# Sparse attention and two dense layers on one core: shifting every SBUF tile to a multiple of 128 bytes

## The chip, the cores and the metric

The kernel runs on one core of one Trainium2 chip. The metric is device time in microseconds (us) of one execution, the median of several runs. TensorE multiplies, VectorE, ScalarE and GpSimd do elementwise work, and SyncE issues almost all transfers. A profile names them PE, DVE, ACT, POOL and SP; PEld is TensorE loading the stationary operand of the next matmul.

## The reference

Attention over 4 batches of 8 heads (576 rows of 64), in which only scores within tau of the row's largest take part, is followed by two dense blocks on the 2304 rows of 512.

```python
scores = scale * np.matmul(q, k.transpose(0, 1, 3, 2))
thresh = np.max(scores, axis=-1, keepdims=True) - tau
scores = np.where(scores >= thresh, scores, -1000000000.0)
attn = softmax(scores)                    # exp, sum + 1e-9, divide
x = np.matmul(attn, v)                    # to rows of 512
h = x @ w_in                              # 512 -> 2048
g = np.maximum(h, 0.0) + alpha * np.minimum(h, 0.0)
x = g @ w_out                             # 2048 -> 512
h = ((x @ w1) * (x @ w2)) @ w3            # 512 -> 1024, 1024 -> 1024
out = h @ w_out2                          # 1024 -> 512
```

The weights arrive as 64-bit floats, and the kernel converts them to 32-bit ones on the chip.

## The kernel before

**Stages.** The attention goes over 16 pairs of heads. For a pair, q and k are loaded (L229, L233), split into a high and a low part (L140, L144, L147, tiles `qs` and `ks`), transposed (L258, L264) into `qT` and `kT`, and `qT` is copied with its halves swapped into `qU` by a transfer (L298). Nine groups of 128 rows follow: four matmuls of 288 columns each (L321), row maximum (L336), exponential (L345), mask (L357), scaling (L380), transposes (L403), and the product with v (L428). Meanwhile 14 of the 16 slices of `w_in` are converted.

The dense part works on five tiles of rows of `x`: four of 512 columns and one of 256, the order being tile 0, the tile of 256, tiles 1 to 3. Every product is made of three matmuls (high by high, high by low, low by high), all by `mm_group` (L819), in a type of 4 bytes that passes through TensorE once. `h<-x,wa` in a profile means that the moving operand is `x` and the stationary one is `wa`; so also `acc<-gs,wu` (second product of the first block), `h<-wu,x` (the product of w3 and w_out2, made once), and `acc<-wp,gs` (the last product). While the first three tiles run, DVE, ACT and POOL convert the other weights (L155 to L177) and put 40 slices of them to DRAM and back.

**Order.** The order of all instructions is made ahead of time by a planner, `list_order`, from estimated costs, and it is fixed in the program: each engine takes its instructions in that order and waits by semaphores. The change leaves the planner and its costs alone.

**Where the tiles lie.** A pool takes a stretch of SBUF from the left or from the right end of what is free, and each tile in it is rounded up to 32 bytes of a partition. Every large tile is a multiple of 128 bytes long, so what stands ahead of the first one sets the remainder of all on that side. On the left the small tiles of `const` (`ident` to `kscale`, L125 to L132) take 1312 bytes from 16512 on, so `xT0` starts at 17824 = 139 x 128 + 32 and the 16 `wa` tiles at 54688 = 427 x 128 + 32, and so on. On the right the free part ends at 229344 = 1791 x 128 + 96, so all tiles of the pools `att`, `dn` and `wu` (`qT`, `kT`, `qU`, `pt`, `x`, `gs`, `wu`, `wp`) start 96 bytes past a multiple of 128. Two operands are at a multiple of 128 already: `ident` (16512) and `ident_r` (17024), the moving operands of the transposes. Between the two sides 576 bytes are free in the dense part, and more than that in the attention.

Of the kernel before, what the change touches and what calls it, by code (L numbers as in the profile page):

```python
# [9 lines left out]
F32 = mybir.dt.float32  # L10
# [73 lines left out]
def kernel(  # L84
# [25 lines left out]
    nc = tc.nc  # L110
# [13 lines left out]
    const = ctx.enter_context(tc.tile_pool(name="const", bufs=1))  # L124
# [7 lines left out]
    kscale = const.tile([128, 1], F32, name="kscale")  # L132

    tiles = [SM] * B + [B * ST]
    xT = [const.tile([128, KD, n], F32, name=f"xT{t}") for t, n in enumerate(tiles)]
    w_a = ctx.enter_context(tc.tile_pool(name="w_a", bufs=16, reuse_waits="tile"))

# [41 lines left out]

    with tc.manual_schedule():  # L180
        make_identity(nc, ident)
        nc.scalar.dma_start(out=tau_sb, in_=tau.partition_broadcast(128))
        nc.scalar.dma_start(out=alpha_sb, in_=alpha.rearrange("(c p) -> p c", p=128))
        nc.vector.tensor_copy(ident_r, ident)
# [905 lines left out]
```

## Time and profile before

| | us |
|---|---|
| median of 3 runs | 1103.19 (1102.81 to 1104.49) |
| the profiled execution, its own time | 1106.0 |
| its span, first to last instruction | 1104.2 |
| PE busy | 1064.2 (96%) |
| DVE busy | 713.5 (65%) |

The span is what the profile's rows add up to; 1.8 us of the profiled execution's time lie around it. The end of a matmul is modelled in the profile, and matmuls overlap, so the distance from the start of one run of matmuls to the start of the next, divided by their number, tells what one costs.

### The profile page before, as it was taken

The page shows a single profiled execution, that of the slowest core. Times are in us where ns is not written, and L with a number is a line of the kernel's source. Part 1 is how long each engine was busy: PE and PEld are TensorE (multiplying, and loading weights), DVE is VectorE, ACT ScalarE, POOL GpSimd, SP SyncE. Part 2 cuts the span into 40 slices and gives each one's busy share as a digit, 9 for nine tenths or more (in the row PEclk, how much of TensorE's full clock was granted, in tenths as well). Part 3 has the DMA queues.
Part 4 walks back from the last instruction along what each step waited for, and adds up shares of the span by engine and source line. Part 5 has one row for each costly group of instructions (what it writes and reads, how often), then busy time and mean ns, then how long its engine had stood idle before and what let it go on. Part 6 is the DMA issues. An engine that isn't in the chain of part 4 may idle for free.

```text
span 1104.2 us, 17783 instructions
## 1 busy us (share of the span) xinstructions
PE 1064.2 (96%) x6464; PEld 891.1 (81%) x6464; DVE 713.5 (65%) x1425; ACT 438.7 (40%) x875; POOL 439.4 (40%) x679
## 2 busy tenths in 40 slices
PE   5999999999999998999989999999999999999997
PEld 5888888888878778978867788888888888888886
DVE  4999999999979999888666635654322312323122
ACT  4888888888874433332333212211110101111020
POOL 5888888888843444454343102301200101000000
PEclk9999999999999998999989999999999999999999
DMA  6443343343213335555434301323100100001010
GB/s 157 123 118 101 102 123 100 107 107 79 60 40 115 108 102 160 175 165 170 124 124 138 101 1 38 97 76 96 48 1 1 39 1 10 29 1 39 1 39 20
DMA packets 62392, 89.25 MB, mean 81 GB/s; under 512 B 13920, under 2 KB 42592, under 8 KB 62304
## 3 DMA queue, kind: packets, MB, share of 16 engines
q1 hardware_dynamic: 60096, 88.10, 27.0%
q8 instruction: 51, 0.84, 0.3%
q10 hardware_dynamic: 2208, 0.01, 0.1%
q14 instruction: 37, 0.30, 0.1%
HBM read 62.40 MB, written 15.20 MB: 70 GB/s over the span
## 4 chain that ended last, share of the span: by engine, by line
PE 65%; DVE 16%; POOL 8%; issue 5%; DMA 3%; ACT 2%; SPq 0%; POOLq 0%; DVEq 0%; ACTq 0%
PE h L819 33%; PE acc L819 21%; POOL p L380 4%; PE s_ps L321 3%; PE pt_ps L403 3%; PE pv_ps L428 3%; DVE p L357 2%; DVE m L172 2%; DVE sm L336 2%; DVE m L168 2%; DMA raw<-in_moe_w_dram 2%; DVE m L166 1%; POOL m L177 1%; DVE g L891 1%; DVE m L163 1%
## 5 line engine op out<-in xcount | busy, mean ns | idle before, releaser
L819 PE MATMUL h<-x,wa 128*128 128x512 f32 (+1 forms) x1920 | 419.7, 371 | 2.7 <-DVE x L147 1.3
L819 PEld LDWEIGHTS h<-x,wa 128*128 128x128 f32 x1920 | 336.0, 189 | 67.9 <-POOL x L147 2.4
L819 PE MATMUL acc<-gs,wu 128*128 128x512 f32 (+1 forms) x960 | 216.8, 374 | 10.7 <-POOL gs L147 5.2
L819 PEld LDWEIGHTS acc<-gs,wu 128*128 128x128 f32 x960 | 169.1, 190 | 47.2 <-POOL gs L147 8.9
L1011 DVE TENSOR_TENSOR ab<-h,ab 128x512 f32<-128x512 f32 (+1 forms) x40 | 25.5, 638 | 207.6 <-PE h L819 201.0
L147 POOL TENSOR_TENSOR x<-xT,x 128x512 fp32r<-128x512 f32 (+1 forms) x18 | 21.6, 1208 | 296.8 <-ACT x L142 249.3
L177 POOL TENSOR_TENSOR m<-m,raw 128x512 int32<-128x512 int32 x58 | 79.4, 1369 | 121.2 <-DVE m L172 90.4
L345 ACT ACTIVATE e<-s_ps,sm 128x576 f32<-128x576 f32 x144 | 108.0, 750 | 37.3 <-DVE sm L336 35.3
L336 DVE TENSOR_REDUCE sm<-s_ps 128x1 f32<-128x576 f32 x144 | 106.0, 744 | 7.3 <-PE s_ps L321 6.9
L1008 ACT COPY ab<-h 128x512 f32<-128x512 f32 (+1 forms) x38 | 20.6, 542 | 223.0 <-PE h L819 220.5
L380 POOL TENSOR_SCALAR p<-p,sm 128x576 f32<-128x576 f32 x128 | 102.9, 808 | 14.4 <-DVE sm L373 10.9
L357 DVE SCALAR_TENSOR_TENSOR p<-s_ps,sm,e 128x576 f32<-128x576 f32 x128 | 103.2, 807 | 6.8 <-ACT e L345 5.1
L819 PE MATMUL acc<-wp,gs 128*128 128x512 f32 x432 | 104.6, 389 | 0.9 <-DVE gs L144 0.9
L886 ACT ACTIVATE g<-h,sign_sb 128x512 f32<-128x512 f32 (+1 forms) x80 | 51.3, 641 | 115.0 <-PE h L819 100.4
L403 PE MATMUL pt_ps<-ident,p 128*128 128x128 f32 x576 | 91.3, 281 | 3.9 <-issue 2.7
L819 PEld LDWEIGHTS acc<-wp,gs 128*128 128x128 f32 x432 | 80.3, 188 | 17.6 <-DVE gs L144 1.1
L428 PE MATMUL pv_ps<-pt,vraw 128*64 128x128 f32 (+1 forms) x1280 | 92.5, 291 | 0.1
L321 PE MATMUL s_ps<-kT,qT 128*128 128x288 f32 x320 | 83.4, 343 | 2.6 <-DVE p L357 1.7
L428 PEld LDWEIGHTS pv_ps<-pt,vraw 128*64 128x64 f32 x1280 | 73.0, 136 | 11.9 <-ACT e L345 4.7
L403 PEld LDWEIGHTS pt_ps<-ident,p 128*128 128x128 f32 x576 | 66.0, 141 | 19.1 <-POOL sm L339 9.2
L891 DVE SCALAR_TENSOR_TENSOR g<-h,salpha_sb,g 128x512 f32<-128x512 f32 (+1 forms) x80 | 55.4, 693 | 39.9 <-ACT g L886 39.7
L415 ACT COPY pt<-pt_ps 128x512 f32<-128x512 f32 x128 | 76.1, 595 | 12.7 <-PE pt_ps L403 10.7
(109 smaller groups left out, 1324.7 us busy)
## 6 DMA issues: line engine op xcount, KB each, us to landing
raw<-in_moe_w_dram SPq DMA_DIRECT2D x32, 512.0 KB, 3.9
raw<-in_moe_w_out_dram SPq DMA_DIRECT2D x24, 512.0 KB, 3.6
qU<-qT SPq DMA_DIRECT2D x32, 320.0 KB, 4.2
z<-w SPq DMA_DIRECT2D x40, 256.0 KB, 2.7
wraw<-in_moe_w_in_dram SPq DMA_DIRECT2D x14, 512.0 KB, 3.8
w<-m SPq DMA_DIRECT2D x24, 256.0 KB, 2.2
qraw<-in_q_dram SPq DMA_DIRECT2D x16, 256.0 KB, 3.2
kraw<-in_k_dram SPq DMA_DIRECT2D x16, 256.0 KB, 2.9
```

What stands on the lines that cost most here:

```text
L177: nc.gpsimd.tensor_tensor(out=mc[0], in0=mc[0], in1=mc[1], op=ALU.add)
L321: nc.tensor.matmul(out=sp[:, j, 0:HS], lhsT=d[t][:, hh, c * 128 : (c + 1) * 128], rhs=d["kT"][:, hh, k0 + j * HS : k0 + (j + 1) * HS], sta ...
L336: nc.vector.tensor_reduce(out=sm[u][:, 0:1], in_=st[u], axis=AX.XY, op=ALU.max, negate=True)
L345: nc.scalar.activation(out=es[u].rearrange("p (j s) -> p j s", j=2), in_=st[u], func=AF.Exp, bias=sm[u][:, 0:1])
L357: nc.vector.scalar_tensor_tensor(out=p.rearrange("p (j s) -> p j s", j=2), in0=st.pop(u), scalar=sm[u][:, 1:2], in1=es.pop(u).rearrange("p ...
L380: nc.gpsimd.tensor_scalar(out=out, in0=in_, scalar1=r, scalar2=1.0, op0=ALU.mult, op1=ALU.mult)
L403: nc.tensor.transpose(t[:, i, :], p[:, at + i * 128 : at + (i + 1) * 128], ident)
L415: nc.scalar.copy(out=pt[:, g, 0:4, 0:128], in_=ps)
L428: nc.tensor.matmul(out=o[64 * hh : 64 * hh + 64, 0:n], lhsT=vr[:, hh, i, :], rhs=pt[:, 0 if i == 4 and c < 3 else hh, i, 0:n], start=(i == 0),
L819: nc.tensor.matmul(out=out, lhsT=l, rhs=r, start=first and i == 0, stop=last and i == n - 1)
L886: nc.scalar.activation(out=gt()[:, 0:n], in_=ps()[:, 0:n], func=AF.Copy, scale=sign_sb[:, f : f + 1])
L891: nc.vector.scalar_tensor_tensor(out=gt()[:, 0:n], in0=ps()[:, 0:n], scalar=salpha_sb[:, f : f + 1], in1=gt()[:, 0:n], op0=ALU.mult, op1=A ...
```

## The change

A tile of 24 elements of 4 bytes, 96 bytes of a partition, that nothing uses is put behind the small tiles of `const`, and a second one, in a pool of its own, at the right end. So the left tiles start 96 bytes later and the right ones 96 bytes earlier: `xT0` at 17920 = 140 x 128, the `wa` tiles from 54784 = 428 x 128 on, and the right side ends at 229248 = 1791 x 128. The right gap is set to zero once, by a GpSimd instruction behind the making of `ident`.

```diff
     tiles = [SM] * B + [B * ST]
+    const.tile([128, 24], F32, name="gap")
+    edge = ctx.enter_context(tc.tile_pool(name="edge", bufs=1, side="right"))
+    gap = edge.tile([128, 24], F32, name="gap_r")
     xT = [const.tile([128, KD, n], F32, name=f"xT{t}") for t, n in enumerate(tiles)]
...
         make_identity(nc, ident)
+        nc.gpsimd.memset(gap, 0.0)
         nc.scalar.dma_start(out=tau_sb, in_=tau.partition_broadcast(128))
```

## Rows read from the trace of the kernel before

**Rows 1.** The page, busy us (share of the span) and instructions of TensorE.

```profile
PE   1064.2 (96%) x6464; PEld 891.1 (81%) x6464; DVE 713.5 (65%) x1425; ACT 438.7 (40%) x875; POOL 439.4 (40%) x679
```

**Rows 2.** Windows: busy us (x instructions) of each engine, granted clock, DMA.

```profile
30.00:327.00 297.00, 291.80 (x2793) 248.95 (x2791) 279.94 (x719) 248.56 (x551) 250.53 (x501) 1.00 0.36 96
327.00:472.00 145.00, 135.74 (x743) 115.38 (x742) 135.30 (x210) 60.36 (x107) 63.42 (x48) 0.98 0.42 131
472.00:630.00 158.00, 150.97 (x680) 121.74 (x681) 113.76 (x176) 49.32 (x81) 64.56 (x48) 0.98 0.44 139
630.00:1090.00 460.00, 460.00 (x2099) 382.25 (x2098) 165.41 (x273) 64.76 (x110) 42.52 (x30) 1.00 0.10 31
```

**Rows 3.** The chain that ended last, 30 to 327 us, by line.

```profile
by line: POOL p L380 14.9%; issue 13.3%; PE pv_ps L428 10.7%; PE s_ps L321 10.7%; PE pt_ps L403 10.4%; DVE p L357 7.8%; DVE sm L336 6.7%; DVE praw L357 3.2%; POOL sm L368 2.9%; POOL ks L140 2.8%; PE tr L264 2.6%; ACT e L345 2.4%; POOL qs L1
```

**Rows 4.** The chain, 327 to 472 us, by line.

```profile
by line: DMA raw<-in_moe_w_dram 13.1%; DVE m L172 12.9%; DVE m L168 9.6%; issue 9.4%; DVE m L166 9.3%; DVE wu L719 8.2%; DVE m L163 7.6%; DVE g L891 7.1%; POOL m L177 7.1%; DVE gs L147 4.6%; DVE gs L144 2.3%; DVE x L147 2.0%; DVE wa L144 1.
```

**Rows 5.** The chain, 472 to 630 us, by line.

```profile
by line: PE h L819 41.5%; PE acc L819 38.7%; PE h L748 4.5%; POOL m L177 2.7%; DVE g L891 1.9%; issue 1.6%; DVE m L166 1.4%; POOL gs L147 1.3%; DVE m L172 1.3%; DVE x L147 1.1%; ACT g L886 0.9%; DVE gs L144 0.9%; DVE m L168 0.8%; DVE m L163
```

**Rows 6.** The chain, 630 to 1090 us, by line.

```profile
by line: PE h L819 65.0%; PE acc L819 35.1%
```

**Rows 7.** Timeline of TensorE, 716 to 731 us: start, us, group.

```profile
722.15 2.88 PE L819 MATMUL acc<-gs,wu 128*128 128x512 f32 x12
724.87 2.91 PE L819 MATMUL h<-x,wa 128*128 128x512 f32 x12
727.62 2.88 PE L819 MATMUL acc<-gs,wu 128*128 128x512 f32 x12
```

**Rows 8.** Timeline of TensorE, 745 to 790 us.

```profile
754.93 5.60 PE L819 MATMUL h<-wu,x 128*128 128x512 f32 x24
760.37 2.88 PE L819 MATMUL acc<-gs,wu 128*128 128x512 f32 x12
```

**Rows 9.** Timeline of TensorE, 434.5 to 440 us, the tile of 256.

```profile
434.42 1.52 PE L819 MATMUL h<-x,wa 128*128 128x256 f32 x12
435.78 1.60 PE L819 MATMUL acc<-gs,wu 128*128 128x256 f32 x12
437.22 1.52 PE L819 MATMUL h<-x,wa 128*128 128x256 f32 x12
```

**Rows 10.** Timeline of TensorE, 140 to 160 us, the scores.

```profile
146.08 0.43 PE L321 MATMUL s_ps<-kT,qT 128*128 128x288 f32 x2
146.35 0.43 PE L321 MATMUL s_ps<-kT,qU 128*128 128x288 f32 x2
146.62 0.60 PE L403 MATMUL pt_ps<-ident,p 128*128 128x128 f32 x4
```

**Rows 11.** Groups by form, TensorE, 472 us to the end: count, busy us, mean ns.

```profile
L819 PE MATMUL h<-x,wa 128*128 128x512 f32 x1344 | 324.5, 395 | 1.7 <-DVE x L147 1.3 <-POOL x L147 0.3
L819 PE MATMUL acc<-gs,wu 128*128 128x512 f32 x576 | 139.1, 391 | 2.0 <-DVE gs L144 1.1 <-POOL gs L147 0.6 <-DVE gs L147 0.2
L819 PE MATMUL acc<-wp,gs 128*128 128x512 f32 x432 | 104.6, 389 | 0.9 <-DVE gs L144 0.9
L819 PE MATMUL h<-wu,x 128*128 128x512 f32 x192 | 43.8, 389 | 0.0
L819 PE MATMUL h<-x,wa 128*128 128x256 f32 x192 | 24.0, 279 | 0.0
```

**Rows 12.** Timeline of TensorE, 1064 to 1076 us, the last tile.

```profile
1066.87 5.81 PE L819 MATMUL h<-x,wa 128*128 128x256 f32 x48
1072.52 1.53 PE L819 MATMUL acc<-wp,gs 128*128 128x512 f32 x6
```

**Rows 13.** Instructions that write `gs` and `x`: ns min/median/max.

```profile
L144 DVE CAST gs<-g x59: 280/429/1541, 336.5 to 752.7; 128x512 fp32r<-128x512 f32 x51, 128x256 fp32r<-128x256 f32 x8
...
L144 DVE CAST x<-xT x19: 282/421/1267, 321.0 to 1059.5; 128x512 fp32r<-128x512 f32 x16, 128x256 fp32r<-128x256 f32 x3
```

**Rows 14.** Timeline of GpSimd, 0 to 22 us: start, us, group, idle before.

```profile
1.36 0.15 POOL L207 MEMSET qraw<- 64x64 f32 x1
...
6.48 0.46 POOL L140 TENSOR_SCALAR qs<-qraw 128x320 fp32r<-128x320 f32 x1 [2.19 <-DMA qraw<-in_q_dram]
```

## The prediction

> **What bounds the kernel.** The page first: TensorE is busy for 96% of the span [rows 1], so what a matmul costs matters, if it is TensorE that sets the end. That differs by stage, so I read windows next and the chain of waits for each. From 30 to 327 us (attention) DVE is nearly as full as PE, 280 us and 292 us of 297 [rows 2], and the chain goes through all engines: the PE lines named there (L428, L321, L403, L264) have 34.4% of it, the scores' matmuls (L321) 10.7% [rows 3]. From 327 to 472 us, in which the first tile and the tile of 256 run, no PE line stands in the part of the chain that is shown: it is the conversion of weights on DVE (135 of 145 us busy [rows 2]) and the loads of weights, 13.1% [rows 4]. From 472 to 630 us PE has 41.5 + 38.7 + 4.5 = 84.7% [rows 5], and from 630 to 1090 us everything [rows 6], at a granted clock of 1.00, the 2.4 GHz level [rows 2]. So a cheaper matmul counts in full over 460 us, mostly over 158 us, and hardly before.
>
> Then I read what one matmul costs, as starts of neighbouring runs. With 512 columns, `acc<-gs,wu` takes (724.87 - 722.15) / 12 = 226.7 ns, `h<-x,wa` 2.75 / 12 = 229.2 ns [rows 7], and `h<-wu,x` 5.44 / 24 = 226.7 ns [rows 8]. With 256 columns, `acc<-gs,wu` takes 1.44 / 12 = 120.0 ns, `h<-x,wa` 1.36 / 12 = 113.3 ns [rows 9] and, in the last tile, 5.65 / 48 = 117.7 ns [rows 12]. The scores' matmuls of 288 columns take 0.54 / 4 = 135 ns [rows 10]. At 2.4 GHz, 226.7 ns is 544 cycles, 120.0 ns is 288, and 135 ns is 324: 32, 32 and 36 more than there are columns.
>
> **Where those 32 cycles may come from.** Columns are 4 bytes wide. A moving operand of 512 columns that starts 96 bytes past a multiple of 128 touches 17 stretches of 128 bytes, where an aligned one would touch 16; 17 times 32 columns is 544. With 256 columns it touches 9 (288 cycles), with 288 columns 10 (320). If a matmul pays for whole stretches, all three sizes come out, and the change removes one stretch from each. But a fixed 32 cycles per matmul, say for handing over the stationary operand, fits the three sizes too. What tips me is a pair: `h<-x,wa` and `h<-wu,x` have the same three passes, the same length and the same kind of output bank, and differ in where the operands lie; in the second both start 96 past, in the first `wa` starts 32 past. Yet they differ, 229.2 against 226.7 ns [rows 7, 8], and with 256 columns `h<-x,wa` differs from `acc<-gs,wu` the other way, 113.3 against 120.0 ns [rows 9]. So time on TensorE does seem to depend on the place within 128 bytes, which the change alters for every operand of the dense products.
>
> The rows show 226.7 ns for 512 columns. The Trainium skill, TensorE: Matmul & The Clock Gate, in its section "Wait — 56ns, not 53.3ns?", gives 215.7 ns for back-to-back matmuls of 512 columns at full clock; this trace does not agree, it is 11.0 ns dearer. By that page the gain per matmul of 512 columns could be 11.0 ns, which changes the sum below by under 1 us.
>
> **The change, part by part.** Nothing in the order of instructions moves, and no wait or transfer is added or taken away.
>
> - The memset of the right gap: one more on GpSimd, behind `ident`. One of 64x64 takes 0.15 us [rows 14]. GpSimd idles 2.19 us before its first work on `qs` [rows 14], waiting for q to land, so I cost it at 0; without that cover it is 0.15 us.
> - Elementwise work: `gs<-g`, whose two tiles start equally far past, and `x<-xT`, whose tiles start 64 bytes apart, have medians of 429 and 421 ns [rows 13]. So I give DVE, ACT and POOL nothing. A gain on DVE would show most before 472 us; the 8 ns between the two medians, over the 929 DVE instructions of 30 to 472 us [rows 2], bound it at 7 us either way.
> - Transfers: the wait for weights is 13.1% of 145 us, 19 us [rows 4]. If shifted destinations made those transfers cheaper or dearer by a tenth, it is 2 us either way; I take 0.
> - Matmuls from 472 us to the end [rows 11]: 576 + 432 + 192 = 1200 at 226.7 ns, 1344 `h<-x,wa` at 229.2 ns, and 192 of 256 columns at 117.7 ns. Between nothing and the 13.3 ns of the 32 cycles I take 10.7 ns, leaving a fifth for a hand-over that no row shows apart. 1200 x 10.7 ns = 12.8 us. For `h<-x,wa` the 2.5 ns that it has beyond the others go too: 1344 x 13.2 ns = 17.7 us. The 256-column ones fall to 106.7 + 2.6 = 109.3 ns: 192 x 8.4 ns = 1.6 us. Together 32.1 us.
> - What of it is lost: a quarter of those 632 us is the stretch from 472 to 630, so 8.0 us of the gain. What is late next there are the conversions that PE already waits for, 15.3% of the chain [rows 5], and a faster PE comes to them sooner. I take off a quarter, 2.0 us; the bounds are 0 and 8.0 us.
> - Matmuls from 327 to 472 us: 743 of them [rows 2], at most 743 x 10.7 ns = 7.9 us. DVE and the loads set the end there [rows 4], so I take 0.
> - Scores: 40 matmuls in each of 16 pairs. Their 10.7% of 297 us on the chain is 32 us [rows 3]; 10.7 of 135 ns is 8%, so 2.5 us at most. I take 1.0 us, since another engine is close behind.
>
> Sum: 32.1 - 2.0 + 1.0 = 31.1 us. The profiled execution took 1106.0 us, so 1074.9 us; it is 2.8 us above the median of 1103.2, so I give 1072 us for the median.
>
> **Rivals.**
>
> - Half a stretch. The 113.3 ns of `h<-x,wa` are 272 cycles, 256 + 16 [rows 9], as if the unit were 64 bytes, and all operands now start 32 past a multiple of 64. Then one unit of 16 cycles, 6.7 ns, goes: 1200 x 6.7 + 1344 x 6.7 + 192 x 6.7 = 18.3 us, 1.2 us lost before 630 us, so 1086 us. Against it: no run of 512 columns in the rows stands at 528 cycles.
> - Only the step between the two operands matters. Then 32 cycles per matmul stay, and `h<-x,wa` comes down to the others, since afterwards all start at the same place: 1344 x 2.5 = 3.4 us less, and 192 x (120.0 - 117.7) = 0.4 us more, so 1100 us. For it speaks that three pairs of operands in step all show 226.7 ns [rows 7, 8].
> - The change does not do what it says, as to time. All tiles already start at multiples of 32 bytes, and if SBUF is read in pieces that divide 32, no piece is saved; the 32 cycles are then a hand-over, and the 2.5 ns of `h<-x,wa` have to do with which pool the operand is in. Then 1103 us. The Trainium skill, SBUF — State Buffer, under "Specifications (TRN2)", speaks for it: it gives cachelines of 16 bytes, at whose multiples all tiles stand before and after. The trace does not clearly agree: `wa`, 32 past, and `wu`, 96 past, are both on such lines, and differ by 2.5 ns.
> - Slower: moving and stationary operands that start at the same multiple of 128 get in each other's way. In step at 96 past they show 226.7 ns, so nothing yet speaks for it; the price is bounded by what being out of step costs now, 2.5 ns. On the 1200 matmuls that lack it, that is 3.0 us, so 1106 us; it decides from 1.8 ns on, 2.2 us. One more stretch for each would be 2736 x 13.3 ns = 36 us.
>
> **How the numbers follow.** About 0.2%, 2.2 us, is what can be told from no change. Full stretch 0.48, half a stretch 0.17, step alone 0.10, nothing 0.15, slower 0.10. The step alone lies at -3 us, so 0.06 of it counts as faster and 0.04 as same. Faster is 0.48 + 0.17 + 0.06 = 0.71, same 0.04 + 0.15 = 0.19, slower 0.10. The likeliest case by itself reaches from 1063 us (all 13.3 ns gone, 7.1 us more, and nothing lost before 630 us) to 1079 us (all 8.0 us lost and no gain at the scores). The range is 1063 to 1103.5 us: it holds nearly all of the first, the next two, and about half of no change, some 0.8.
>
> **What would show it right or wrong.** Right: runs of 512 columns at 214 to 217 ns in the timeline, equal for `h<-x,wa`, `h<-wu,x` and `acc`; 256 columns at 107 to 110 ns, 288 at 121 to 125 ns; the first 472 us nearly as long as before, with more idle PE from 327 to 472 us. A pitch of 220 ns says half a stretch, 226.7 everywhere says step alone. If pitches fall and the span does not, the bound has moved to the conversions, and PE's idle time before L819 grows by what was saved. The forecast fails most simply if 32 cycles stay.

## The result: 0.6% slower

The changed kernel takes 1110.78 us (median of 5 runs, 1110.36 to 1111.24) against 1104.49 us for the kernel before in the same series; the ratio is 1.0057, with a 95% interval of 1.0040 to 1.0074. The profiled execution took 1110.9 us, with a span of 1109.1 us, 4.9 us more than before. Each engine's instructions stand in the same order as before, with the one memset added.

The page of the changed kernel, TensorE's line, as [rows 1]:

```profile
PE   1071.5 (97%) x6464; PEld 892.5 (80%) x6464; DVE 714.0 (64%) x1425; ACT 439.3 (40%) x875; POOL 439.6 (40%) x680
```

PE has the same 6464 matmuls and is busy 7.3 us longer; DVE, ACT and POOL have changed by less than 1 us. Next the last two of the windows, as [rows 2]: us, busy us (x instructions) of PE, PEld, DVE, ACT and POOL, granted clock, DMA.

```profile
472.00:630.00 158.00, 152.23 (x681) 122.12 (x681) 114.21 (x174) 49.22 (x80) 63.24 (x47) 0.98 0.42 139
630.00:1090.00 460.00, 460.00 (x2057) 377.86 (x2057) 163.73 (x269) 63.90 (x108) 42.44 (x30) 1.00 0.10 31
```

The granted clock is that of before in all four windows of [rows 2]. In the three up to 630 us as many matmuls are done as before, to within 3 (2790, 746 and 681). In the 460 us in which nothing but PE stands on the chain, 2057 matmuls fit where 2099 did [rows 2], so on average one got dearer. Which ones did, the timeline of TensorE tells (start, us, group), as [rows 7, 8 and 12]:

```profile
622.32 5.82 PE L823 MATMUL h<-x,wa 128*128 128x512 f32 x24
...
719.53 2.96 PE L823 MATMUL h<-x,wa 128*128 128x512 f32 x12
722.33 2.92 PE L823 MATMUL acc<-gs,wu 128*128 128x512 f32 x12
725.08 2.96 PE L823 MATMUL h<-x,wa 128*128 128x512 f32 x12
...
750.09 5.63 PE L823 MATMUL acc<-gs,wu 128*128 128x512 f32 x24
755.56 5.60 PE L823 MATMUL h<-wu,x 128*128 128x512 f32 x24
761.00 2.88 PE L823 MATMUL acc<-gs,wu 128*128 128x512 f32 x12
...
921.27 2.90 PE L823 MATMUL acc<-wp,gs 128*128 128x512 f32 x12
924.01 5.75 PE L823 MATMUL h<-x,wa 128*128 128x512 f32 x24
...
1071.24 5.93 PE L823 MATMUL h<-x,wa 128*128 128x256 f32 x48
1077.01 1.56 PE L823 MATMUL acc<-wp,gs 128*128 128x512 f32 x6
...
1102.22 1.66 PE L823 MATMUL acc<-wp,gs 128*128 128x512 f32 x6 [0.91 <-DVE gs L147]
```

The same view of the kernel before, where [rows 7, 8 and 12] do not show it:

```profile
623.61 5.75 PE L819 MATMUL h<-x,wa 128*128 128x512 f32 x24
...
918.97 2.88 PE L819 MATMUL acc<-wp,gs 128*128 128x512 f32 x12
921.69 5.66 PE L819 MATMUL h<-x,wa 128*128 128x512 f32 x24
927.18 2.88 PE L819 MATMUL acc<-wp,gs 128*128 128x512 f32 x12
...
1097.29 1.66 PE L819 MATMUL acc<-wp,gs 128*128 128x512 f32 x6 [0.92 <-DVE gs L144]
```

Starts are printed to 0.01 us, so the pitch (the time from one matmul's start to the next) is known to 0.8 ns from a run of 12 and to 0.4 ns from one of 24; less than that is not read. From start to start, `h<-x,wa` went from 229.2 to (722.33 - 719.53) / 12 = 233.3 ns, and with 256 columns from 117.7 to 5.77 / 48 = 120.2 ns. `h<-wu,x`, whose operands now both start at a multiple of 128, is at 5.44 / 24 = 226.7 ns, where it was. `acc<-gs,wu` went from 226.7 to 2.75 / 12 = 229.2 ns, but in a run of 24 it is at 5.47 / 24 = 227.9 ns: some 30 ns per run, however long it is. It is paid where `acc` follows a run of `h<-x,wa`, and is not `acc`'s own: between two runs of `h<-wu,x`, from 761.00 to 763.72 us, `acc<-gs,wu` is at 226.7 ns.

This accounts for the time. From the start of a run of 24 `h<-x,wa` (623.61 us before, 622.32 us now; it stands on the chain in both) to that of TensorE's last run (1097.29 and 1102.22 us), called the *tail* below, it was 473.7 us and is 479.9 us: 6.2 us more, as the medians say (6.3 us). That the run starts 1.3 us earlier now says nothing of the change: in both_shift below, which has the pitches of before, it starts at 619.58 us, and in right_only at 624.30 us. In the tail of before are 1056 `h<-x,wa` of 512 columns (x 4.1 ns = 4.3 us), 300 `acc<-gs,wu` (x 2.5 = 0.8), 432 `acc<-wp,gs` (2.74 / 12 = 228.3 now, 226.7 before; x 1.6 = 0.7) and 192 `h<-x,wa` of 256 columns (x 2.5 = 0.5): 6.3 us together.

### The profile page after: what moved, and what is told of

Its sections match the earlier page's. It is cut to its first block, busy times and chain, and to the rows that moved or that the text cites. A ratio compares the mean times of both kernels' runs of the same rounds, so it can differ in the third digit from the quotient of the medians.

```text
span 1109.1 us, 17784 instructions
## 1 busy us (share of the span) xinstructions
PE 1071.5 (97%) x6464; PEld 892.5 (80%) x6464; DVE 714.0 (64%) x1425; ACT 439.3 (40%) x875; POOL 439.6 (40%) x680
## 4 chain that ended last, share of the span: by engine, by line
PE 61%; DVE 17%; POOL 9%; issue 6%; DMA 4%; ACT 3%; SPq 0%; POOLq 0%; DVEq 0%; ACTq 0%
PE h L823 33%; PE acc L823 20%; POOL p L384 4%; DMA raw<-in_moe_w_dram 3%; DVE p L361 3%; PE s_ps L325 2%; PE pv_ps L432 2%; DVE sm L340 2%; PE pt_ps L407 2%; DVE m L175 2%; DVE m L171 2%; POOL m L180 2%; DVE m L169 2%; DVE g L895 1%; DVE wu L723 1%
## 5 line engine op out<-in xcount | busy, mean ns | idle before, releaser
L823 PE MATMUL h<-x,wa 128*128 128x512 f32 (+1 forms) x1920 | 426.4, 375 | 2.6 <-DVE x L150 1.3
```

The source lines that it names most:

```text
L823: nc.tensor.matmul(out=out, lhsT=l, rhs=r, start=first and i == 0, stop=last and i == n - 1)
```

## The experiments

Two theories, and the names that the expectations use: D, the pitch of a matmul depends on the *distance* between the places of its moving and its stationary operand; P, it depends on the *place* of an operand within 128 bytes. In bytes, x - wa (for the `wa` tile at the lowest place) was 139840 = 546 x 256 + 64 before, and is 139648 = 545 x 256 + 128 after; gs - wu, wp - gs and wu - x are multiples of 256 in both.

**staircase.** Each `wa` tile is 32 bytes longer than it needs to be, so that the 16 tiles lie at 16 distances, 8 of them different modulo 256.

```diff
-            wa[f] = w_a.tile([128, 2, KD, 128], F32R, tag="wa", name="wa")
+            w = w_a.tile([128, 1032], F32R, tag="wa", name="wa")
+            wa[f] = w[:, 0:1024].rearrange("p (a k f) -> p a k f", a=2, k=KD)
...
-                box["w"] = pool.tile([128, 2, 512], F32R, tag=tag, name=tag, **kw)
+                if pool is w_a:
+                    w = pool.tile([128, 1032], F32R, tag=tag, name=tag, **kw)
+                    box["w"] = w[:, 0:1024].rearrange("p (a f) -> p a f", a=2)
+                else:
+                    box["w"] = pool.tile([128, 2, 512], F32R, tag=tag, name=tag, **kw)
```

> Each stationary tile of w_in lies 32 bytes further from the one ahead of it than before, so slice f starts 576 - 32f bytes below x (modulo 4096); x, gs, wu and wp stay where they were. Theory D (what counts is the distance between the moving and the stationary operand): the pitch of h<-x,wa differs from slice to slice; 229 ns at f = 0 (distance 576 as before), 226.7 ns at f = 2 (distance 512), 233 ns at f = 6 (distance 384 as after the change); others unknown. Theory P (what counts is where an operand starts within 128 bytes): the pitch repeats with every fourth slice, and the slices that start at a multiple of 128 (f = 3, 7, 11, 15) are the slow ones at 233 ns.

I had the order of the tiles wrong: the pool gives the first slice its lowest place and the next ones its places from the top down, so slice f lies at a distance of 64 + 32f, modulo 256, and not 576 - 32f; the addresses in the program as it was built are these. The expectation is to be read with that order, and what the staircase says for D hangs on it: by the order that was expected, slice 2 would lie at 0 and slice 6 at 128. in_step, further down, tests the distance 0 without it. Timeline of TensorE in one tile of rows, the slices 2, 6, 7 and 8 (the run of `acc` that follows each gives its end):

```profile
675.37 2.96 PE L824 MATMUL h<-x,wa 128*128 128x512 f32 x12
678.16 2.92 PE L824 MATMUL acc<-gs,wu 128*128 128x512 f32 x12
...
697.53 2.88 PE L824 MATMUL h<-x,wa 128*128 128x512 f32 x12
700.25 2.89 PE L824 MATMUL acc<-gs,wu 128*128 128x512 f32 x12
702.98 2.95 PE L824 MATMUL h<-x,wa 128*128 128x512 f32 x12
705.77 2.88 PE L824 MATMUL acc<-gs,wu 128*128 128x512 f32 x12
708.49 2.91 PE L824 MATMUL h<-x,wa 128*128 128x512 f32 x12
711.23 2.89 PE L824 MATMUL acc<-gs,wu 128*128 128x512 f32 x12
```

Slice 6 (distance 0) takes 2.72 / 12 = 226.7 ns, slice 8 (64) 228.3 ns, slice 2 (128) 232.5 ns, slice 7 (32) 232.5 ns; in the same way slices 3, 4, 5 and 9 (160, 192, 224, 96) take 232.5 to 233.3 ns. Slice 10 is at 232.5 ns as slice 2, and 11 and 12 at 233.3 ns as 3 and 4: the pattern repeats after 8 slices, 256 bytes. Theory P wanted it to repeat after four. One execution, 1109.5 us.

**in_step, left_only, both_shift.** The first line of each diff stands ahead of `xT`; both_shift has the memset of the change too.

```diff
+    const.tile([128, 144], F32, name="gap")       # in_step: 576 bytes on the left
...
+    const.tile([128, 24], F32, name="gap")        # left_only: 96 bytes on the left
...
+    const.tile([128, 8], F32, name="gap")         # both_shift: 32 on the left, 480 on the right
+    edge = ctx.enter_context(tc.tile_pool(name="edge", bufs=1, side="right"))
+    gap = edge.tile([128, 120], F32, name="gap_r")
```

> One gap of 576 bytes on the left alone, none on the right: wa starts 96 past a multiple of 128 and x - wa is a multiple of 4096; nothing on the right moves. Theory D: h<-x,wa falls from 229.2 to 226.7 ns as the other products, some 1344 x 2.5 = 3.4 us after 472 us, so about 1101 us. Theory P: wa at 96 past, as wu is, gives the same 226.7 ns; this run alone does not part the two, but it says whether the step is worth what either says.

> The left gap of the change alone: wa at a multiple of 128, x, gs, wu, wp where they were; x - wa is 480 bytes modulo 4096. Theory D: a pitch of h<-x,wa that is that of distance 480, neither 229.2 nor 233 of necessity, and acc<-gs,wu by itself still settles at 226.7. Theory P: h<-x,wa has half of what the change cost, about 231 ns, and acc stays at 226.7 throughout; some 1107 us.

> A left gap of 32 and a right gap of 480 bytes: x, gs, wu, wp all start at a multiple of 128 as after the change, and x - wa is 64, which is 576 as before less 512. Theory D: pitches as before, 229.2 for h<-x,wa and 226.7 for the others, and a time of 1103 to 1105 us. Theory P: the right side, aligned, costs what it did after the change, acc<-gs,wu near 229 and h<-x,wa over 231 ns, 1107 us or more.

| | median us | ratio to before | 95% interval | tail, us (before 473.7) |
|---|---|---|---|---|
| in_step | 1102.65 | 0.9986 | 0.9977 to 0.9995 | 471.9 |
| left_only | 1110.34 | 1.0059 | 1.0044 to 1.0075 | 479.0 |
| both_shift | 1103.22 | 0.9991 | 0.9981 to 1.0000 | 473.7 |

Timeline of TensorE in in_step, then in left_only, then in both_shift:

```profile
718.17 2.88 PE L820 MATMUL h<-x,wa 128*128 128x512 f32 x12
720.89 2.88 PE L820 MATMUL acc<-gs,wu 128*128 128x512 f32 x12
```

```profile
719.54 2.96 PE L820 MATMUL h<-x,wa 128*128 128x512 f32 x12
722.33 2.89 PE L820 MATMUL acc<-gs,wu 128*128 128x512 f32 x12
```

```profile
720.84 2.91 PE L823 MATMUL h<-x,wa 128*128 128x512 f32 x12
723.59 2.88 PE L823 MATMUL acc<-gs,wu 128*128 128x512 f32 x12
726.31 2.91 PE L823 MATMUL h<-x,wa 128*128 128x512 f32 x12
...
750.90 5.60 PE L823 MATMUL h<-wu,x 128*128 128x512 f32 x24
756.34 2.88 PE L823 MATMUL acc<-gs,wu 128*128 128x512 f32 x12
```

In step, `h<-x,wa` is at 226.7 ns as everything else. With the left gap alone it is at 232.5 ns, and the kernel already as slow as with the whole change, although only `wa` and `xT` were moved. In both_shift everything on the right lies at a multiple of 128, as after the change, and all pitches are those of before: 229.2, 226.7 and 226.7 ns. So alignment by itself costs nothing and gives nothing, and P falls. in_step is faster than both kernels, by 1.5 us of the 3.4 expected (0.6 to 2.5 us by the interval); its tail is 1.8 us shorter. The 3.4 us counted 1344 matmuls from 472 us on, of which 1056 stand in the tail (x 2.5 = 2.6 us), and left out that those of 256 columns get dearer: a run of 48 of them, from 1063.83 to 1069.58 us, is at 119.8 ns for 117.7, 192 x 2.1 = 0.4 us.

**right_only.** The other half of the change.

```diff
+    edge = ctx.enter_context(tc.tile_pool(name="edge", bufs=1, side="right"))
+    gap = edge.tile([128, 24], F32, name="gap_r")
...
+        nc.gpsimd.memset(gap, 0.0)
```

> The right gap of the change alone, with its memset: x, gs, wu, wp at a multiple of 128, wa and xT where they were; x - wa is 480, or 224 modulo 256, the same distance as with the left gap alone. Theory D: the same as with the left gap alone, h<-x,wa at 233 ns in the long stretches, h<-wu,x at 226.7, acc only raised behind a run of h, about 1110 us. Theory P: the opposite half of the change from left_only, so acc<-gs,wu, acc<-wp,gs and h<-wu,x change and h<-x,wa keeps part of its 229 ns; another time than left_only's 1110.

It took 1109.97 us, a ratio of 1.0047 (1.0031 to 1.0064). Its timeline:

```profile
721.12 2.96 PE L822 MATMUL h<-x,wa 128*128 128x512 f32 x12
723.92 2.90 PE L822 MATMUL acc<-gs,wu 128*128 128x512 f32 x12
...
757.00 5.60 PE L822 MATMUL h<-wu,x 128*128 128x512 f32 x24
762.44 2.88 PE L822 MATMUL acc<-gs,wu 128*128 128x512 f32 x12
```

`h<-x,wa` takes 233.3 ns, `h<-wu,x` 226.7 ns, `acc` 227.5 ns, as with the left gap alone to within a nanosecond, and the tail is 479.0 us in both: either gap makes the distance 224, modulo 256, and nothing else of them shows.

**wu_off.** D as a forecast for other operands: 160 bytes between two pools on the right, nothing aligned.

```diff
+        step = ctx.enter_context(tc.tile_pool(name="step", bufs=1, side="right"))
+        gap = step.tile([128, 40], F32, name="gap_s")
+        nc.gpsimd.memset(gap, 0.0)
         wu_pool = ctx.enter_context(tc.tile_pool(name="wu", bufs=16, side="right", reuse_waits="tile"))
```

> The kernel before with 160 bytes put between the pool of x and gs and that of wu and wp. Nothing is aligned; only distances change: gs - wu from 0 to 160 modulo 256, wp - gs and wu - x from 0 to 96; x - wa stays 64. Theory D, with the staircase's values as a table: acc<-gs,wu 234.4 ns, acc<-wp,gs and h<-wu,x 233.5 ns, h<-x,wa 229.2 as before; after 472 us 576 x 7.7 + 432 x 6.8 + 192 x 6.8 = 8.7 us more, so about 1113 us. Theory P: wu starts 64 past a multiple of 128 instead of 96, gs stays; all pitches within 1 to 2 ns of before, at most 1106 us.

It took 1114.52 us against 1104.59 us, a ratio of 1.0089 (1.0072 to 1.0106): 9.9 us more, where 8.7 were expected. Its timeline:

```profile
722.63 2.98 PE L822 MATMUL acc<-gs,wu 128*128 128x512 f32 x12
725.44 2.92 PE L822 MATMUL h<-x,wa 128*128 128x512 f32 x12
728.20 2.97 PE L822 MATMUL acc<-gs,wu 128*128 128x512 f32 x12
...
756.09 5.77 PE L822 MATMUL h<-wu,x 128*128 128x512 f32 x24
761.70 2.96 PE L822 MATMUL acc<-gs,wu 128*128 128x512 f32 x12
...
923.72 2.95 PE L822 MATMUL acc<-wp,gs 128*128 128x512 f32 x12
926.51 5.76 PE L822 MATMUL h<-x,wa 128*128 128x512 f32 x24
932.10 2.95 PE L822 MATMUL acc<-wp,gs 128*128 128x512 f32 x12
```

`acc<-gs,wu` is at 2.81 / 12 = 234.2 ns (234.4 expected), `h<-wu,x` at 5.61 / 24 = 233.8 (233.5), `acc<-wp,gs` at 232.5 (233.5). What D did not expect: `h<-x,wa`, whose distance is still 64, is at 2.76 / 12 = 230.0 ns between the runs of `acc<-gs,wu`, and at 5.59 / 24 = 232.9 ns between those of `acc<-wp,gs`. So at this distance a run can go at 229 or at 233 ns, and which one depends on what ran ahead of it, though not on the distance of that run alone: behind `h<-wu,x`, at 96 as `acc<-wp,gs` is, a run of 48, from 803.70 to 814.69 us, goes at 229.0 ns. The tail is 483.0 us, 9.3 us more than before. The runs at 233 ns are 720 matmuls of it, x 4.1 = 3.0 us that were not expected; with 300 `acc<-gs,wu` (x 7.5 = 2.3), 432 `acc<-wp,gs` (x 5.8 = 2.5) and 192 `h<-wu,x` (x 7.1 = 1.4) that makes 9.1 us. That the expectation came out as near as 8.7 us is in part luck: it left these 3.0 us out, and counted 276 `acc<-gs,wu` (2.1 us) that run before the tail, where PE alone does not set the time.

**staircase_odd.** The staircase, 16 bytes further in.

```diff
-            wa[f] = w[:, 0:1024].rearrange("p (a k f) -> p a k f", a=2, k=KD)
+            wa[f] = w[:, 4:1028].rearrange("p (a k f) -> p a k f", a=2, k=KD)
```

> The staircase with the stationary operand taken 16 bytes further into each tile: distances modulo 256 of 48 + 32f. Theory D with a collision of whole 32-byte or larger pieces: pitches lie between those of the neighbouring distances, 226.6 nowhere or at two distances next to 0. If there is a distance at which the two reads miss each other, some slice falls below 226 ns, towards the 213 ns of 512 columns; then the 32 cycles are a collision too and not a hand-over.

Timeline, the slices 2, 6 and 7:

```profile
675.65 2.88 PE L824 MATMUL h<-x,wa 128*128 128x512 f32 x12
678.37 2.89 PE L824 MATMUL acc<-gs,wu 128*128 128x512 f32 x12
...
697.71 2.88 PE L824 MATMUL h<-x,wa 128*128 128x512 f32 x12
700.43 2.88 PE L824 MATMUL acc<-gs,wu 128*128 128x512 f32 x12
703.15 2.88 PE L824 MATMUL h<-x,wa 128*128 128x512 f32 x12
705.87 2.88 PE L824 MATMUL acc<-gs,wu 128*128 128x512 f32 x12
```

Distances 112, 240 and 16 (slices 2, 6, 7) are at 226.7 ns, the others above: 80 at 230.0 ns, 48 and 176 at 231.7, 144 and 208 at 233.3. So of 16 distances in steps of 16 bytes, four are free (0, 16, 112, 240) and 64 is nearly so. 112, between 96 and 128, is not between its neighbours, so the expectation's picture of pieces of 32 bytes fails. And no slice falls below 226.7 ns. 112 depends on what runs ahead as well: where a slice at 80 runs directly ahead, the three runs at 112 take 233.2 to 234.2 ns (from 807.04, 939.23 and 1005.32 us). One execution, 1108.0 us.

**narrow.** What are the 32 cycles that stay? In every twelve matmuls of `h<-x,wa` the stationary operand is cut to 64 columns in three and to 32 in three; the rows of `h` that these leave out lack their share.

```diff
+    const.tile([128, 144], F32, name="gap")
...
-            mm_group(
-                ps()[:, 0:n],
-                [(wt()[:, wp, kc], xs[kc]()[:, xp, 0:n]) for kc in range(KD) for wp, xp in PASSES],
-            )
+            wide = (128, 64, 32, 128)
+            for kc in range(KD):
+                c = wide[kc]
+                mm_group(
+                    ps()[0:c, 0:n],
+                    [(wt()[:, wp, kc, 0:c], xs[kc]()[:, xp, 0:n]) for wp, xp in PASSES],
+                    kc == 0,
+                    kc == KD - 1,
+                )
```

> in_step, with h<-x,wa in the second of its four k steps made with 64 and in the third with 32 stationary columns instead of 128, so that part of h lacks half and three quarters of their share (output not the reference's). Theory L (the 32 cycles that remain in step are the price of the stationary load going on beside the moving read): the matmul that runs beside a load of 64 columns takes about 220 ns, beside one of 32 about 217 ns. Theory H (a fixed hand-over): 226.7 ns whatever is loaded.

By L, a run of 12 would take 6 x 226.7 + 3 x 220 + 3 x 217 = 2671 ns, by H 2720 ns. Its timeline (one execution, 1102.6 us):

```profile
926.49 2.90 PE L820 MATMUL h<-x,wa 128*128 128x512 f32 x12
929.23 2.88 PE L820 MATMUL acc<-wp,gs 128*128 128x512 f32 x12
...
1063.27 5.83 PE L820 MATMUL h<-x,wa 128*128 128x256 f32 x48
1068.94 1.55 PE L820 MATMUL acc<-wp,gs 128*128 128x512 f32 x6
```

It takes 2.74 us, so with 512 columns a run is no cheaper, and L's forecast fails. H's, 226.7 ns whatever is loaded, fails too. Matmul by matmul (the median over the 85 or 86 such runs after 630 us), the six narrow ones are 224 to 236 ns from the next start, where all twelve of in_step are 226 or 227 ns. And with 256 columns a run is cheaper: 5.67 / 48 = 118.1 ns, against 119.8 in in_step. So the width of the stationary operand changes the pitch at an unchanged distance. As a narrower one also makes fewer rows of output, which of the two does it is not shown, and what the 32 cycles are stays open.

## Why the prediction was wrong

**The bound was right.** From 630 us on PE alone is on the chain, and an added nanosecond per matmul counts in full there (6.3 us summed, 6.2 us found). How much of it counts between 472 us and the tail, no run here shows: it would be 2 us at most (288 `h<-x,wa` x 4.1 ns and 276 `acc<-gs,wu` x 2.5 ns), and the start of the tail differs by more than that between before and both_shift, which have the same pitches. The chain from 472 to 630 us of the changed kernel does not tell either:

```profile
by line: PE h L823 36.6%; PE acc L823 32.3%; DMA raw<-in_moe_w_dram 6.8%; POOL m L180 5.2%; PE h L752 3.2%; issue 3.1%; DVE m L169 2.1%; DVE g L895 1.9%; DVE m L175 1.3%; ACT raw L158 1.3%; DVE x L150 1.1%; DVE gs L147 0.9%; ACT g L890 0.8%
```

PE has 72.1% where it had 84.7% [rows 5], but in both_shift, with the pitches of before, it has 35.1 + 30.4 + 2.9 = 68.4% in that stretch, so the change need not be the cause.

**The step that failed** is "If a matmul pays for whole stretches, all three sizes come out, and the change removes one stretch from each". Operands at a multiple of 128 still take 226.7 ns (`h<-wu,x` after the change and in both_shift). At 512 columns the 32 cycles stay wherever the operands are aligned, as the other reading, a fixed cost, would have it (that it is fixed for every size is not shown: 256 columns are at 113.3 to 120.2 ns, 16 to 32 cycles above their number). In place of gains of 12.8, 17.7 and 1.6 us the tail shows losses of 1.5 us (0.8 + 0.7), 4.3 and 0.5 us, and the 1.0 us for the scores, taken from the same 10.7 ns, goes with them.

**What tipped me was read too narrowly.** The pair `h<-x,wa` and `h<-wu,x` did show that places matter [rows 7, 8]. I concluded "the place within 128 bytes"; the rows said as well that the two pairs differ in the distance between the operands, which was 64 in the one and 0 in the other. in_step, both_shift, left_only and right_only show that the distance counts and the place does not; wu_off adds that at a distance of 64 the run ahead counts too.

**The right rival had the wrong sign.** "Only the step between the two operands matters" was the mechanism. I gave it -3 us "since afterwards all start at the same place", that is, modulo 128. Left tiles moved up by 96 and right ones down by 96, so the distance fell by 192, from 576 to 384 (modulo 4096, the length of one tile), which is 0 modulo 128 but 128 modulo 256; and the period is 256, as the staircase shows. At 128 the pitch is 232.5 to 233.3 ns, against 228.3 to 229.2 ns at 64. For the dense products the rows of before held only the distances 0 and 64 and could not tell the period (of the three pairs in step that the rival counts, [rows 7, 8] show two; the third, `acc<-wp,gs`, is at 226.7 ns too); what was missing was to say that 384 is a distance of which no row shows the price. The rival in which it is slower named operands in step as the danger; those remained the cheap ones.

**The pages.** The Trainium skill, SBUF — State Buffer, under "Specifications (TRN2)", gives lines of 16 bytes, by which nothing should have changed; as to alignment the runs agree with it (both_shift: 0.9991); that the distance counts, that line does not say. The Trainium skill, TensorE: Matmul & The Clock Gate, under "Step-by-step: what each phase is for", says that loading the next tile's weights does not steal read bandwidth of SBUF from the running matmul. The measurement does not fit that, and decides: by the distance between the two operands the same matmul took 226.7 to 234.2 ns. That it is the load of the *next* matmul that meets the running one is argued from their overlap and from narrow, where the width of the stationary operand changed the pitch, and is not shown by itself.

## What to carry to other kernels

Where TensorE is the bound and operands are 4 bytes wide, as here, look at the distance between the moving and the stationary operand, not at the alignment of either: pools that grow from two ends, or a small tile ahead of large ones, set it by accident. Here 576 bytes of unused space, which put all pairs of the dense products a multiple of 256 apart, made the kernel 0.14% faster, and 96 bytes at either end 0.5 to 0.6% slower. And when rows show that two groups differ, list everything in which they differ before one of these becomes the mechanism, and ask of each what it makes of the new case.

## What the runs showed of the hardware that was not expected

- The pitch of a 512-column matmul as a function of the distance between its operands, modulo 256 bytes: 226.7 ns at 0, 16, 112 and 240; 228.3 to 229.2 at 64; 230.0 at 80; 231.7 at 48 and 176; 232.5 to 234.2 at the rest, which are 32, 96, 128, 144, 160, 192, 208 and 224 (behind runs that are in step, or nearly so, except in wu_off). With 256 columns it goes differently: 120.0 ns at 0, and 113.3 or 117.7 ns at 64 [rows 9, 12], and 118.3 or 120.2 ns at 128.
- What came before counts: behind a run of `h<-x,wa` after the change, a run of `acc<-gs,wu` costs some 30 ns more, whether it has 12 or 24 matmuls, and at the distance 64 a run of 24 kept 232.9 ns throughout in wu_off, where the same run takes 5.49 / 24 = 228.8 ns in the kernel before. At 112, 226.7 ns became 233.2 to 234.2 ns directly behind a slice at 80.
- No matmul run of 512 columns, at any distance, alignment or width of the stationary operand tried here, went below 226.7 ns at full granted clock, 32 cycles more than its columns. Single matmuls in narrow did (224 ns), beside others at 236 ns. What those cycles are stays open.
